# Memory attention plus a long convolution on one core: an evacuation engine chosen by the scheduler, masks as products in the last segment, and a tail without zero blocks

## The chip, the cores and the metric

The kernel runs on one core of one Trainium2 chip. The metric is the device time of one execution in microseconds (us). Three runs of the kernel before took 506.79, 511.01 and 514.14 us; the median is 511.01 us. The engines that matter are TensorE (PE, with its weight loads shown as PEld), VectorE (DVE), ScalarE (ACT) and SyncE (SP), which issues every DMA. GpSimd (POOL) does a few memsets.

## The reference

The input x has 2048 tokens of 512 numbers. Two branches are computed from x and mixed by a gate per token. All weights are bfloat16.

```python
g = sigmoid((x * gate_w).sum(-1, keepdims=True))
# A: 32 heads of 16, N = 4 segments of L = 512 tokens
logits = einsum('bhqd,bhkd->bhqk', qs, ks) * scale + mask      # per segment, causal
a_dot = einsum('bhqk,bhkd->bhqd', softmax(logits), vs)
a_mem = (phi(qs) @ M) / (phi(qs) @ z + 1e-6)                   # phi(t) = t+1 if t>0 else exp(t)
o = gh * a_mem + (1 - gh) * a_dot                              # gh = sigmoid(beta), per head
M, z = M + phi(ks)^T vs, z + sum(phi(ks))                      # carried to the next segment
a = o @ wo
# B: a state-space convolution; K from 128 complex states per channel
P = exp(dt * (A_re + 1j*A_im) * l)                             # l = 0..2047
K = einsum('dn,dnl,dn->dl', Cc, P, dB).real
b = irfft(rfft(pad(x)) * rfft(pad(K)))[:2048] + x * Dskip
out = g * a + (1 - g) * b
```

## The kernel before

Every engine instruction and DMA is an `Op` with a key (its due time), an engine, a cost and the tiles that it reads, writes and needs. `Sched.schedule` (L252) places all of them before the launch: it repeatedly takes, for each engine, the ready op with the lowest key that could start soon, and appends it to that engine's program. The result is one fixed order per engine. On the chip each engine runs its list in order and waits for semaphores; an instruction that waits holds up everything behind it on its engine. All DMAs are in one such list, on SP, issued at L249. All matmuls but the transposes are recorded at L720.

The keys come from `KEYS = (12, 6, 50, 70)` (L17): attention groups are due 12 apart from 6 on, the tables of the convolution start at 50 and are 70 apart, and the tail is due after the fourth table.

The pieces, with the lines that the text speaks of:

- **Powers** (`ssm_prep`, `ssm_powers`, L773 to L833): ACT and DVE square a complex number ten times, one step after the other, and store each power in the pool `pw`.
- **Attention** (L923 to L1117). Per segment of 512 tokens: V is projected and copied out of PSUM (L936); q and k are projected per group of 8 heads (`project`; q copied at L984, k twice with a head mask at L987 and L988). A `group` (L999) is 4 heads. It has 5 slots: 2 or 4 score products with 32 rows each; then 2 products of the identity with a block `negm` that adds -30000 above the diagonal (L1026); one exp on ACT over 128x1024 (L1032); and the products with V (17 columns) that add into `PV`, which is copied to `raw` (L1046). There are 32 groups, so 160 exps. `ophase` (L1051) transposes, normalises on DVE, adds the memory part and copies `oT` (L1099). `oproj` (L1102) multiplies by wo, scales by the gate (L1115) and writes `scr_abuf` to DRAM.
- **Gates** (`gate_tokens`, L897): after segment 3 the gate column goes to DRAM (`scr_gbuf`) and comes back in another layout; DVE reads it at L916.
- **Tables** (`tables(c)`, four times): 15 complex multiplies of three DVE instructions each (L1148, L1150, L1153) fill F and G with powers; 256 small products on PE (32 rows by 49 columns) make K samples, copied by ACT (L1195), written to `scr_K` in four DMAs and read back as one (L1199); DVE shuffles them (L1200, L1203), PE transposes them into `KTT`, ACT copies (L1213).
- **First Fourier step of x** (`x_level1`): products copied by ACT (L879) and DVE (L881) and written to `scr_Z`.
- **Tail** (`tail`, L1216). The constants `c_M2` and `c_N1` (2 MB each) and `scr_Z` are loaded (32 DMAs). Then 16 steps t: load a slice `c_D`; 10 products make K's spectrum (L1246), ACT copies (L1250); 16 products of 64 rows by 64 columns over 256 (L1261) make x's spectrum, ACT copies (L1267); DVE multiplies (L1271, L1273, L1275); 4 products with N1 (L1282) transform back; DVE or ACT in turn copy V (L1286, L1288) and it goes to `scr_V`. After every fourth t, `scr_V` is read back transposed into V2 by four DMAs (L1294).
- **End** (`fin`, L1298): four times: load x and `scr_abuf` pieces, u = x*Dskip on DVE (L1310), per quarter an identity product of u and two products with G2 and V2 (L1318 to L1320), one DVE instruction that mixes (L1324), four DMAs out.

Buffers that share memory belong to phases: Zx, M2, N1 and the rest of the tail's pools lie over F, G, t2 and `pw` (L686 to L695), and a pool can be used only when all pools under it are finished.

## Time and profile before

| | |
|---|---|
| runs | 506.79, 511.01, 514.14 us (median 511.01) |
| the profiled execution's own time | 510.9 us |
| its span | 509.1 us |
| mean granted clock of TensorE | 0.837 |
| PE busy | 376.7 us (74%), 3801 matmuls |
| DVE busy | 341.1 us (67%), 586 instructions |
| ACT busy | 310.8 us (61%), 397 instructions |
| DMA | 46.02 MB in 64489 packets |
| chain that ended last, by engine | PE 31%, DVE 28%, DMA 17%, ACT 12%, SP's queue 6%, issue 4% |

Read the shares of busy time as averages over stages with different limits: none of the engines is busy all the time, and each stage has its own one that ends last. [...] In a row of the timeline the brackets give how long the engine had been idle before and what released it.

### The profile page before, as it was taken

Reading aid. Unit: us, or ns where it says so; the run is one execution under the profiler, and the core shown is the slowest. Engines: PE = TensorE matmul, PEld = TensorE weight load, DVE = VectorE, ACT = ScalarE, POOL = GpSimd, SP = SyncE. Lnnn points to the kernel's source line nnn. Section 1 sums busy time; section 2 is a strip of 40 time slices with the busy share of each in tenths; the row PEclk is TensorE's granted clock in tenths of the full one; section 3 lists DMA queues with packets and bytes.
Section 4 is the critical chain, followed back from the end, with each engine's and each line's share of the span. In section 5 each row is a group of like instructions: output and inputs, shape, how many; then the busy total and the mean of one; then the engine's idle time right before and its main releaser. Section 6 shows DMA issues by size and latency. Waiting matters only on the chain.

```text
span 509.1 us, 9111 instructions
## 1 busy us (share of the span) xinstructions
PE 376.7 (74%) x3801; PEld 165.1 (32%) x3837; DVE 341.1 (67%) x586; ACT 310.8 (61%) x397; POOL 4.5 (1%) x17
## 2 busy tenths in 40 slices
PE   4873499999667976889877789647991898985370
PEld 3330133334333425334333233223341344432010
DVE  3777586999576897899965999432120878664074
ACT  4899986978556883586884639624581266554000
POOL 1000000000000000000000000000000000000000
PEclk9995555999895996999995989966587799999586
DMA  8600003222491101200015000059999757654546
GB/s 234 159 1 2 0 0 128 80 84 88 133 52 44 42 0 18 49 1 33 12 16 42 10 3 1 1 154 190 214 152 181 165 169 215 194 179 146 154 111 160
DMA packets 64489, 46.02 MB, mean 90 GB/s; under 512 B 28353, under 2 KB 59585, under 8 KB 64193
## 3 DMA queue, kind: packets, MB, share of 16 engines
q1 hardware_dynamic: 64448, 45.44, 40.2%
q8 instruction: 30, 0.49, 0.5%
q14 instruction: 11, 0.08, 0.1%
HBM read 31.23 MB, written 14.20 MB: 89 GB/s over the span
## 4 chain that ended last, share of the span: by engine, by line
PE 31%; DVE 28%; DMA 17%; ACT 12%; SPq 6%; issue 4%; DVEq 0%; ACTq 0%
PE psum L720 29%; SPq L249 6%; DVE sb L1153 5%; DVE sb L1150 5%; DVE sb L1148 4%; ACT sb L1032 3%; DMA scr_K<-sb 3%; DMA sb<-in_A_x_dram 2%; DMA scr_gbuf<-sb 2%; DMA scr_abuf<-sb 2%; DMA sb<-c_D 2%; ACT sb L819 2%; DMA sb<-scr_V 2%; DMA sb<-scr_K 1%; DVE sb L881 1%
## 5 line engine op out<-in xcount | busy, mean ns | idle before, releaser
L720 PE MATMUL psum<-sb 128*32 128x49 bf16 (+15 forms) x3565 | 357.1, 292 | 92.1 <-ACT sb L1032 17.1
L720 PEld LDWEIGHTS psum<-sb 128*128 128x128 bf16 (+5 forms) x3601 | 146.1, 101 | 298.3 <-issue 125.5
L1032 ACT ACTIVATE sb<-psum 128x1024 bf16<-128x1024 f32 x160 | 158.0, 1028 | 40.0 <-PE psum L720 38.5
L1153 DVE TENSOR_TENSOR sb<-sb 128x2048 bf16<-128x2048 bf16 (+3 forms) x60 | 51.8, 864 | 1.8
L1148 DVE TENSOR_TENSOR sb<-sb 128x2048 bf16<-128x2048 bf16 (+3 forms) x60 | 51.2, 857 | 0.1
L1150 DVE TENSOR_TENSOR sb<-sb 128x2048 bf16<-128x2048 bf16 (+3 forms) x60 | 51.3, 855 | 0.0
L1250 ACT ACTIVATE sb<-psum 128x1024 bf16<-128x1024 f32 x16 | 16.4, 1023 | 24.2 <-PE psum L720 24.2
L1115 ACT ACTIVATE sb<-psum,sb 128x512 bf16<-128x512 f32 x16 | 11.0, 687 | 24.5 <-PE psum L720 17.4
L1310 DVE TENSOR_TENSOR sb<-sb 128x2048 bf16<-128x2048 bf16 x4 | 9.1, 2289 | 19.4 <-PE psum L720 18.8
L1046 ACT ACTIVATE sb<-psum 128x512 bf16<-128x512 f32 x32 | 19.1, 597 | 2.8 <-PE psum L720 2.8
L1267 ACT ACTIVATE sb<-psum 128x1024 bf16<-128x1024 f32 x16 | 16.2, 1021 | 4.6 <-PE psum L720 4.6
L1064 DVE RECIPROCAL sb<-psum 128x32 f32<-128x32 bf16 x16 | 5.6, 352 | 19.4 <-PE psum L1059 19.4
L1059 PE MATMUL psum<-sb 128*128 128x128 bf16 x128 | 12.9, 260 | 7.2 <-ACT sb L1115 6.0
L1286 DVE CAST sb<-psum 128x1024 bf16<-128x1024 f32 x8 | 9.8, 1224 | 11.9 <-PE psum L720 11.9
L988 DVE TENSOR_SCALAR sb<-psum,sb 128x512 bf16<-128x512 f32 x16 | 11.9, 745 | 6.5 <-ACT sb L987 6.5
L1099 DVE CAST sb<-psum 128x512 bf16<-128x512 f32 x16 | 11.0, 687 | 7.4 <-PE psum L720 7.4
L1195 ACT ACTIVATE sb<-psum 128x392 bf16<-128x392 f32 x16 | 7.4, 501 | 13.5 <-PE psum L720 11.1
L881 DVE CAST sb<-psum 128x1024 bf16<-128x1024 f32 x8 | 9.8, 1223 | 7.0 <-PE psum L720 6.8
L1324 DVE SCALAR_TENSOR_TENSOR sb<-psum,sb 128x512 bf16<-128x512 f32 x16 | 10.8, 742 | 4.6 <-DMA out_dram<-sb 4.6
L1083 DVE TENSOR_SCALAR sb<-psum 128x32 f32<-128x32 f32 x12 | 2.2, 186 | 17.3 <-PE psum L720 17.3
L1059 PEld LDWEIGHTS psum<-sb 128*128 128x128 bf16 x128 | 10.5, 120 | 9.5 <-ACT sb L1115 6.2
L987 ACT ACTIVATE sb<-psum,sb 128x512 bf16<-128x512 f32 x16 | 11.0, 689 | 4.2 <-PE psum L720 4.1
(83 smaller groups left out, 257.4 us busy)
## 6 DMA issues: line engine op xcount, KB each, us to landing
sb<-c_D SPq DMA_DIRECT2D x16, 320.0 KB, 4.6
sb<-in_A_x_dram SPq DMA_DIRECT2D x32, 128.0 KB, 4.5
scr_Z<-sb SPq DMA_DIRECT2D x16, 256.0 KB, 2.1
sb<-scr_Z SPq DMA_DIRECT2D x32, 128.0 KB, 8.8
scr_V<-sb SPq DMA_DIRECT2D x16, 256.0 KB, 3.6
sb<-scr_V SPq DMA_DIRECT2D x16, 256.0 KB
sb<-in_A_x_dram SPq DMA_DIRECT2D x4, 512.0 KB, 4.3
scr_abuf<-sb SPq DMA_DIRECT2D x16, 128.0 KB, 2.6
```

The source lines that it names most:

```text
L249: return self.op("SP", 0.06, lambda e: e.dma_start(out(), in_(), **kw), r=r, w=w, pw=pw, key=key, lat=lat)
L720: mm = lambda e, o_, l, r_, st, sp, **kw: e.matmul(o_, lhsT=l, rhs=r_, start=st, stop=sp, skip_group_check=True, **kw)
L881: op("DVE", c_dps(1024), lambda e, P=P, zs=zs: e.tensor_copy(ap(zs, n=1024), ap(P, n=1024)), r=[P], w=[zs])
L988: op("DVE", c_dps(512), lambda e, P=P: e.tensor_scalar(ap(ko, n=512), ap(P, n=512), ap(mkT, 1, n=1), None, ALU.mult), r=[P, mkT], w=[ko])
L1032: op("ACT", c_act(1024), lambda e, P=P, pT=pT: e.activation(ap(pT, n=1024), ap(P, n=1024), ACT.Exp, scale=0.25), r=[P], w=[pT])
L1046: op("ACT", c_act(512), lambda e: e.activation(ap(raw, n=512), ap(PV, n=512), ACT.Copy), r=[PV], w=[raw])
L1059: i = e.transpose(ap(P, tb * 256 + gi * 128, n=128), ap(ra[gi], tb * 128, n=128), ap(ident, n=128))
L1148: op("DVE", c_tt(256 * n), lambda e: e.tensor_tensor(run(tile, ne, dst, 1), run(tile, ne, src, sstep), pwv(0), ALU.mult), r=rd + [pw], w=w ...
L1150: op("DVE", c_tt(256 * n), lambda e: e.tensor_tensor(run(t2, n, 0, 1), run(tile, ne, src, sstep), pwv(1), ALU.mult), r=rd + [pw], w=[t2])
L1153: op("DVE", c_tt(256 * n), lambda e: e.tensor_tensor(D_(), D_(), ap(t2, n * 128, [[-n * 128, 2], [2 * n, 64], [1, 2 * n]]), ALU.add), r=[t ...
L1250: op("ACT", c_act(1024), lambda e, PK=PK, K3=K3: e.activation(ap(K3, dims=[[1024, 2], [1, 512]]), ap(PK, dims=[[512, 2], [1, 512]]), ACT.C ...
L1267: op("ACT", c_act(1024), lambda e, PX=PX, Xs=Xs: e.activation(ap(Xs, dims=[[256, 2], [512, 2], [1, 256]]), ap(PX, dims=[[512, 2], [256, 2] ...
```

## The change

1. Copies out of PSUM that had a fixed engine (xT, parameters, V, q, both k, zs, `PV`, `oT`, the `oproj` result, kex, KTT, and in the tail K3, Xs, V) become ops with two alternatives (`evac`): the scheduler puts each on ACT or DVE while it builds the order. DVE's alternative carries a key 20 higher (`PEN`).
2. In the last segment (all 8 groups, `MASKD = 24`) the identity products that add `negm` are gone. After the exp a DVE multiply by a 0/1 block zeroes the masked parts of `pT` in place (40 multiplies).
3. The tail's data are laid out anew. M2 and N1 lose their zero blocks (1 MB each). `scr_Z` is loaded so that one product over 128 rows replaces two over 64: 4 products of 64 output columns over 512 in place of 16 over 256. The back transform becomes 8 products of 64x64 over 512, in pairs on the two diagonal quadrants, in place of 4 full ones. V goes to `scr_V` by two DMAs of 64 partitions per t, in runs of 1 KB, and comes back by two DMAs of 16 partitions per four t, in place of four of 8.
4. M2, N1 and the small tail buffers move over `pw`; the `c_D` slices move over G. There are 4 `c_D` slots (3 before), 3 Xs, 3 Y and 5 V.
5. `KEYS` are (11, 6, 60, 65). Some costs given to the scheduler change, and PE ops now acquire the destination tile of the copy that follows.

```diff
-KEYS = (12, 6, 50, 70)
+KEYS = (11, 6, 60, 65)
+    def evac(self, dst, src, n, r, w=(), pw=(), key=None, scale=None, psum16=False):
+        if scale is None:
+            fa = lambda e: e.activation(dst(), src(), ACT.Copy)
+            fd = lambda e: e.tensor_copy(dst(), src())
...
+        return self.op("ANY", 0.0, None, r=r, w=w, pw=pw, key=key,
+                       alts={"ACT": (0.17 + 0.000833 * n + ex, fa), "DVE": (0.15 + (0.00052 if psum16 else 0.00104) * n + ex / 2, fd)})
...
+        def push(o):
+            if o.alts:
+                for e_ in o.alts:
+                    ready[e_].append((o.key + (PEN if e_ == "DVE" else 0.0), o.seq, o))
...
         ZxP = mkpool("Zx", 32768, 1, 2)
-        M2P = mkpool("M2", 16384, 1, 2)
-        N1P = mkpool("N1", 16384, 1, 2)
-        DP = mkpool("Dst", 2560, 3, 2)
+        DP = mkpool("Dst", 2560, 4, 2)
+        a = T1
+        M2P = mkpool("M2", 8192, 1, 2)
+        N1P = mkpool("N1", 8192, 1, 2)
...
+            md = 8 * s + 2 * hg + gi >= MASKD
...
-                    for bk in range(2):
+                    for bk in (() if md else range(2)):
...
+                if md:
...
+                    op("DVE", c_tt(128 * len(offs)), lambda e, pT=pT, dims=dims: e.tensor_tensor(
+                        ap(pT, dims=dims + [[1, 128]]), ap(pT, dims=dims + [[1, 128]]),
+                        ap(mask01, dims=[[0, k_[1]] for k_ in dims] + [[1, 128]]), ALU.mult), r=[mask01], w=[pT])
...
-                for h in range(2):
-                    for i in range(4):
-                        S.dma(lambda h=h, i=i, zq=zq: ap(Zx, zq * 4096, [[256, 16], [1, 256]], p0=64 * h + 16 * i, np_=16),
-                              lambda h=h, i=i, zq=zq: bass.AP(Zd, zq * 16 * 2048 + i * 512 + h * 256, [[256 * 512, 16], [2048, 16], [1, 256]]),
+                for i in range(4):
+                    for c in range(2):
+                        S.dma(lambda c=c, i=i, zq=zq: sbp(Zx, 64 * c + i, 4, 16, [[512, 8], [1, 512]], zq * 4096),
+                              lambda c=c, i=i, zq=zq: bass.AP(Zd, zq * 8 * 4096 + c * 2048 + i * 512, [[256 * 512, 16], [4096, 8], [1, 512]]),
...
-                        for ci in range(2):
-                            for pi in range(2):
-                                for h in range(2):
-                                    p = 2 * t + pi
-                                    i = mm(e, ap(PX, h * 512 + co * 256, n=256, p0=64 * pi, np_=64),
...
+                        for pi in range(2):
+                            p = 2 * t + pi
+                            i = mm(e, ap(PX, co * 512, n=512, p0=64 * pi, np_=64), ap(M2, p * 128 + co * 64, n=64),
+                                   ap(Zx, p * 512, n=512), True, True, tile_position=(0, 64 * pi))
...
-                            i = mm(e, ap(PI, co * 512, n=512), ap(N1, ((t * 2 + ci) * 2 + co) * 128, n=128), ap(Y, ci * 512, n=512), ci == 0, ci == 1)
+                            for pi in range(2):
+                                cx = co if pi == 0 else 1 - co
+                                i = mm(e, ap(PI, cx * 512, n=512, p0=64 * pi, np_=64), ap(N1, ((t * 2 + ci) * 2 + cx) * 64, n=64, p0=64 * pi, np_=64),
+                                       ap(Y, ci * 512, n=512, p0=64 * pi, np_=64), ci == 0, ci == 1, tile_position=(64 * pi, 64 * pi))
...
+                for pi in range(2):
+                    S.dma(lambda t=t, pi=pi: bass.AP(Vd, (2 * t + pi) * 65536, [[512, 64], [32768, 2], [1, 512]]),
+                          lambda V=V, pi=pi: ap(V, dims=[[512, 2], [1, 512]], p0=64 * pi, np_=64), 131072, r=[V], pw=[dV[t // 4]])
...
-                        for c in range(2):
-                            S.dma(lambda bl=bl, c=c, k=k: sbp(V2, 64 * bl + 32 * c + k, 4, 8, [[512, 32], [1, 512]]),
-                                  lambda bl=bl, c=c, k=k: bass.AP(Vd, k * 4 * 131072 + bl * 1024 + c * 512, [[65536, 8], [2048, 32], [1, 512]]),
-                                  262144, r=[dV[k]], pw=[V2])
+                        S.dma(lambda bl=bl, k=k: sbp(V2, 64 * bl + k, 4, 16, [[512, 32], [1, 512]]),
+                              lambda bl=bl, k=k: bass.AP(Vd, k * 8 * 65536 + bl * 512, [[32768, 16], [1024, 32], [1, 512]]),
+                              524288, r=[dV[k]], pw=[V2])
```

What the scheduler makes of it is seen in the engines' lists. The first place is SP's list from the copies of the last `oproj` of segment 2 to the read of the fourth table's K samples (`sb<-scr_K`); before the change it is

```order
L249 DMA sb<-c_D 128x1280 x3
L249 DMA sb<-c_N1 128x8192
L249 DMA scr_abuf<-sb 128x512
L249 DMA scr_K<-sb 128x8x49 x3
L249 DMA sb<-c_M2 128x8192
L249 DMA sb<-scr_Z 16x16x256 x8
L249 DMA scr_K<-sb 128x8x49
L249 DMA sb<-scr_Z 16x16x256 x15
L249 DMA scr_abuf<-sb 128x512
L249 DMA sb<-scr_Z 16x16x256 x9
L249 DMA sb<-scr_K 128x1568
```

and with the change, in the same place,

```order
L252 DMA sb<-c_M2 128x4096
L252 DMA sb<-c_N1 128x4096
L252 DMA scr_K<-sb 128x8x49 x3
L252 DMA sb<-c_D 128x1280 x2
L252 DMA sb<-scr_Z 16x8x512 x7
L252 DMA scr_K<-sb 128x8x49
L252 DMA sb<-scr_Z 16x8x512 x25
L252 DMA sb<-c_D 128x1280 x2
L252 DMA sb<-scr_K 128x1568
```

All 32 loads of `scr_Z` still stand ahead of the read of `scr_K`, each with 128 runs of 1 KB in place of 256 of 512 B; the two constants, half as long, come before the K samples are written.

The second place is SP's list at the end, from the last V writes to the first results; before:

```order
L249 DMA scr_V<-sb 128x1024 x4
L249 DMA scr_abuf<-sb 128x512 x2
L249 DMA sb<-scr_V 8x32x512 x4
L249 DMA scr_abuf<-sb 128x512 x2
L249 DMA sb<-scr_abuf 32x4x512 x12
L249 DMA out_0_dram<-sb 32x4x512 x4
```

and with the change:

```order
L252 DMA scr_V<-sb 64x2x512 x2
L252 DMA scr_abuf<-sb 128x512 x2
L252 DMA scr_V<-sb 64x2x512 x2
L252 DMA sb<-scr_abuf 32x4x512 x8
L252 DMA scr_V<-sb 64x2x512 x4
L252 DMA sb<-scr_V 16x32x512 x2
L252 DMA sb<-scr_abuf 32x4x512 x4
L252 DMA out_0_dram<-sb 32x4x512 x4
```

Eight of the sixteen `scr_abuf` loads now stand ahead of the last V writes; before, all stood behind the last V read.

The third place is DVE's list around the gate column of segment 3 (L910, L911 and L916 before; L929, L930 and L935 now). Before:

```order
L910 TENSOR_SCALAR sb<-sb 128x4
L911 RECIPROCAL sb<-sb 128x4
L1153 TENSOR_TENSOR sb<-sb 128x128x16
L1099 CAST sb<-psum 128x512
L1148 TENSOR_TENSOR sb<-sb 128x128x16
L1150 TENSOR_TENSOR sb<-sb 128x2048
L1153 TENSOR_TENSOR sb<-sb 128x128x16
L916 TENSOR_SCALAR sb<-sb 128x16
```

and with the change:

```order
L1060 TENSOR_TENSOR sb<-sb 128x2x128
L1060 TENSOR_TENSOR sb<-sb 128x2x2x128
L1060 TENSOR_TENSOR sb<-sb 128x2x128
L1060 TENSOR_TENSOR sb<-sb 128x2x2x128
L1060 TENSOR_TENSOR sb<-sb 128x4x128
L1177 TENSOR_TENSOR sb<-sb 128x128x8
L1179 TENSOR_TENSOR sb<-sb 128x1024
L1182 TENSOR_TENSOR sb<-sb 128x128x8
L1012 TENSOR_SCALAR sb<-sb 128x512
L1013 TENSOR_SCALAR sb<-sb 128x512
L1177 TENSOR_TENSOR sb<-sb 128x128x8
L935 TENSOR_SCALAR sb<-sb 128x16
```

L929 and L930 stand directly ahead of these rows. The five masks of a group (L1060) stand in DVE's list one behind the other, and the reader of the gate column still stands a few instructions behind its producer.

## Rows read from the trace of the kernel before

**Rows 1.** Stretches: busy us (count) of PE, PEld, DVE, ACT, POOL; clock; DMA share; GB/s

```profile
0.00:63.50 63.50, 36.31 (x257) 16.84 (x263) 39.59 (x80) 54.78 (x82) 2.15 (x9) 0.81 0.32 79
63.50:337.00 273.50, 221.68 (x2470) 98.15 (x2492) 221.95 (x373) 185.83 (x237) 2.37 (x8) 0.86 0.21 40
...
344.50:385.60 41.10, 36.78 (x297) 14.93 (x296) 9.15 (x25) 25.55 (x30) 0.00 (x0) 0.68 1.17 180
385.60:397.60 12.00, 0.73 (x6) 0.59 (x7) 2.27 (x9) 0.70 (x1) 0.00 (x0) 0.58 1.08 177
397.60:466.50 68.90, 60.30 (x454) 27.11 (x461) 50.67 (x79) 37.53 (x39) 0.00 (x0) 0.97 0.61 181
466.50:478.90 12.40, 2.34 (x11) 0.88 (x9) 0.00 (x0) 2.59 (x4) 0.00 (x0) 0.76 0.45 148
478.90:509.10 30.20, 13.25 (x47) 3.47 (x48) 15.30 (x18) 0.00 (x0) 0.00 (x0) 0.73 0.55 139
```

**Rows 2.** Groups by form: a table multiply of 512 elements, and the exp

```profile
L1150 DVE TENSOR_TENSOR sb<-sb 128x512 bf16<-128x512 bf16 x8 | 3.4, 422 | 0.0
...
L1032 ACT ACTIVATE sb<-psum 128x1024 bf16<-128x1024 f32 x160 | 158.0, 1028 | 40.0 <-PE psum L720 38.5
```

**Rows 3.** Timeline of DVE: start, us, instruction, [idle before and its releaser]

```profile
335.04 0.18 DVE L916 TENSOR_SCALAR sb<-sb 128x16 f32<-128x16 f32 x1 [11.01 <-DMA sb<-scr_gbuf]
```

**Rows 4.** Timeline of SP's queue, from the fourth table's K writes to their read

```profile
341.51 7.41 SPq L249 DMA_DIRECT2D scr_K<-sb  x3
...
349.57 11.81 SPq L249 DMA_DIRECT2D sb<-scr_Z  x8
...
363.82 12.60 SPq L249 DMA_DIRECT2D sb<-scr_Z  x15
...
385.03 1.18 SPq L249 DMA_DIRECT2D sb<-scr_K  x1
```

**Rows 5.** Timeline of DVE: the first reader of those K samples

```profile
394.87 0.16 DVE L1200 COPY sb<-sb 128x1 bf16<-128x1 bf16 x1 [9.11 <-DMA sb<-scr_K]
```

**Rows 6.** DMA issues on SP: ns least/median/most, first and last start

```profile
L249 SPq DMA_DIRECT2D sb<-scr_Z x32: 440/680/6124, 349.6 to 383.9; - x32
L249 SPq DMA_DIRECT2D sb<-in_A_x_dram x10: 312/432/433, 386.2 to 399.5; - x10
...
L249 SPq DMA_DIRECT2D sb<-scr_V x16: 639/652/762, 420.1 to 470.8; - x16
```

**Rows 7.** Timeline of weight loads in a group of segment 3: mask, then V product

```profile
357.45 0.13 PEld L720 LDWEIGHTS psum<-sb 128*128 128x128 bf16 x2 [0.41 <-issue]
...
357.98 0.09 PEld L720 LDWEIGHTS psum<-sb 128*17 128x17 bf16 x2 [0.41 <-issue]
```

**Rows 8.** Timeline of PE and its weight loads in the tail's 16 steps

```profile
412.24 0.36 PEld L720 LDWEIGHTS psum<-sb 64*64 64x64 bf16 x16 [0.42 <-issue]
...
412.80 1.84 PEld L720 LDWEIGHTS psum<-sb 128*128 128x128 bf16 x10 [0.20 <-issue]
...
416.12 7.22 PE L720 MATMUL psum<-sb 128*128 128x512 bf16 x59 [0.42 <-DVE sb L1275]
...
449.96 6.57 PE L720 MATMUL psum<-sb 128*128 128x512 bf16 x56 [1.41 <-DMA sb<-c_D]
```

**Rows 9.** Timeline of the end: V's last read, weight loads, the mixing

```profile
468.71 2.75 SPq L249 DMA_DIRECT2D sb<-scr_V  x4
...
478.91 2.28 PE L720 MATMUL psum<-sb 128*128 128x512 bf16 x6 [10.07 <-DMA sb<-scr_V]
...
483.89 0.10 PEld L720 LDWEIGHTS psum<-sb 128*128 128x128 bf16 x1 [0.23 <-issue]
484.21 0.11 PEld L720 LDWEIGHTS psum<-sb 128*64 128x64 bf16 x2 [0.23 <-issue]
...
488.19 5.35 DVE L1324 SCALAR_TENSOR_TENSOR sb<-psum,sb 128x512 bf16<-128x512 f32 x8
...
500.83 2.73 DVE L1324 SCALAR_TENSOR_TENSOR sb<-psum,sb 128x512 bf16<-128x512 f32 x4 [1.38 <-DMA out_dram<-sb]
```

More of the change, by code (lines that the diff above doesn't have):

```diff
@@ L128 @@
     __slots__ = ("eng", "cost", "fn", "deps", "key", "tiles", "wt", "nd", "succ", "start", "fin", "idx", "inc",
-                 "val", "sem", "know", "waits", "seq", "lat", "alld", "tag")
+                 "val", "sem", "know", "waits", "seq", "lat", "alld", "tag", "alts")
 class Sched:
@@ L335, in schedule @@
             o = choice[e][3]
-            ready[e].remove((o.key, o.seq, o))
+            if o.alts:
+                for e_ in o.alts:
+                    ready[e_] = [r_ for r_ in ready[e_] if r_[2] is not o]
+                o.eng = e
+                o.cost, o.fn = o.alts[e]
+            else:
+                ready[e].remove((o.key, o.seq, o))
             for T in o.tiles:
@@ L491, in fft_consts @@
     cs, sn = np.cos(th), np.sin(th)
-    rows = np.array([4 * b4 + i for i in range(4) for b4 in range(16)])
     m2 = np.zeros((64, 32, 2, 2, 64))
@@ L497, in fft_consts @@
     m2[:, :, 1, 1, :] = cs.transpose(1, 0, 2)
-    m2 = m2[rows]
-    M2 = np.concatenate([m2, m2], 0)
-    N1 = np.zeros((128, 16, 2, 2, 128))
+    M2 = m2.transpose(2, 0, 1, 3, 4).reshape(128, 32, 2, 64)
+    N1 = np.zeros((128, 16, 2, 2, 64))
     for t in range(16):
@@ L960, in f @@
                         return i
-                    op("PE", c_mm(136, 8), f, r=[vpad[s]] + [t for tb in range(4) for t in ekr[(s, tb)]], pw=[P])
+                    op("PE", c_mm(136, 8), f, r=[vpad[s]] + [t for tb in range(4) for t in ekr[(s, tb)]], pw=[P], acq=[Mx[s + 1]])
                 acc = lambda hp=hp: ap(accT, hp * 272, n=272)
@@ L1028, in f @@
                     return i
-                cost = 0.30 + 0.06 * len(ent)
                 pT = Tile(pTP, BF16)
-                op("PE", cost, f, r=[qT, ke, ko, ident, negm], w=[P], acq=[pT])
+                op("PE", 0.33 if md else 0.63, f, r=[qT, ke, ko, ident, negm], w=[P], acq=[pT])
                 op("ACT", c_act(1024), lambda e, P=P, pT=pT: e.activation(ap(pT, n=1024), ap(P, n=1024), ACT.Exp, scale=0.25), r=[P], w=[pT])
+                if md:
+                    offs = [bk * 512 + off for (_, _, bk, off) in ent]
+                    if len(offs) == 2:
+                        dims = [[512, 2]]
+                    elif 384 in offs:
+                        dims = [[512, 2], [384, 2]]
+                    else:
+                        dims = [[512, 2], [256, 2]]
+                    op("DVE", c_tt(128 * len(offs)), lambda e, pT=pT, dims=dims: e.tensor_tensor(
+                        ap(pT, dims=dims + [[1, 128]]), ap(pT, dims=dims + [[1, 128]]),
+                        ap(mask01, dims=[[0, k_[1]] for k_ in dims] + [[1, 128]]), ALU.mult), r=[mask01], w=[pT])
                 def g(e, pT=pT, ent=ent, seen0=dict(seen)):
@@ L1098, in ophase @@
             op("PE", c_mm(128, 4 * len(srcs)), f3, r=srcs + [ident], w=[P3], acq=[oT])
-            op("DVE", c_dps(512), lambda e: e.tensor_copy(ap(oT, n=512), ap(P3, n=512)), r=[P3], w=[oT])
+            S.evac(lambda: ap(oT, n=512), lambda: ap(P3, n=512), 512, r=[P3], w=[oT])
             oTs[(s, hg)] = oT
@@ L1329, in tail, with sbp @@
                           lambda ou=ou, i=i: ap(ou, p0=32 * i, np_=32, dims=[[512, 4], [1, 512]]), 131072, r=[ou])
-        def sbp(T, p0, pstep, np_, dims):
+        def sbp(T, p0, pstep, np_, dims, off=0):
             v = S.sb16[:]
@@ L1334, in sbp @@
             base = (T.pool.addr + T.slot * T.pool.size) // 2
-            return bass.AP(v.tensor, v.offset + p0 * st + base, [[pstep * st, np_]] + [list(d) for d in dims])
+            return bass.AP(v.tensor, v.offset + p0 * st + base + off, [[pstep * st, np_]] + [list(d) for d in dims])
         S.key = 0.0
```

113 lines of the change are left out of this document (53 added, 60 removed).

## Prediction

> **What bounds the kernel now.** I read the busy time by stretches first [rows 1], then, inside each stretch, the timeline of the engine that ends it. All times are of the profiled execution: 509.1 us of span, 510.9 us with what lies around it, against a median of 511.01 us, so the sum can be made against 510.9. Five stretches matter.
>
> (a) 0 to 63.5 us: ACT is busy 54.78 of 63.5 us with the powers, one after the other; DVE has 24 us free. (b) 63.5 to 337 us, the four tables with most of the attention under them: DVE is busiest in sum (221.95 of 273.5 us), PE equals it (221.68), ACT has 88 us free. The largest single gap is DVE's 11.01 us at L916, which waits for the gate column to come back from DRAM with everything on DVE behind it [rows 3]. (c) 341.5 to 397.6 us: the fourth table's K samples are written from 341.51 us on and are read by DVE only at 394.87 us [rows 4, 5], because their read stands in SP's queue behind 32 loads of `scr_Z`. PE works off the rest of the attention until 385.6 us at a granted clock of 0.68, and then is busy 0.73 of 12 us [rows 1]. (d) 397.6 to 466.5 us, 16 tail steps: PE is busy 60.30 of 68.9 us at a clock of 0.97; two steps take 7.22 + 0.42 = 7.64 us [rows 8], so PE is the bound. (e) 466.5 us to the end: PE waits 10.07 us for the last V read; the products start at 478.91 us, but the mixing instruction L1324 starts only at 488.19 us [rows 9], since the `scr_abuf` loads stand behind that read in SP's queue.
>
> **The change, part by part**
>
> *Copies on either engine, new keys, and the masks on DVE* (stretches a and b). By the order, DVE has between the first table's first copy and the last table multiply 27 copies out of PSUM where it had 55, and 25 of the 40 mask multiplies, which are new. At the stretch's mean of 221.95/373 = 0.60 us, 28 fewer copies are 17 us; most are larger than the mean, say 20 us. A mask has 256 or 512 elements; 25 at up to 0.42 us [rows 2] are 10 us. A few more normalisations bring 2 us. DVE's work falls by 8 us. Fifteen copies more come before the tables, into DVE's 24 free us of stretch a. ACT takes over about 28 copies and, by the order, 10 exps more before the table products end (150 against 140): some 17 + 10 us against 88 us free. PE gets 10 slots more and 25 mask steps less. So stretch b ends 8 us earlier if DVE bounds it. The unknown is how a new order of 9,000 instructions fits: DVE's free time in b is 51.5 us, 11 of it the wait for the gate column, which stays (the new order has 12 instructions between producer and reader). If half of the other 40 us went, the gain would be 8 + 20 = 28; if DVE fitted half as badly again, the loss would be 12. I take -8, ends -20 and +12.
>
> *scr_Z in longer runs* (stretch c). SP needs 0.68 us for one `scr_Z` load of 256 runs and 0.652 for one `scr_V` read of 256 runs, but 0.432 for an x load of 128 [rows 6]. The new loads have 128 runs. From the first K write to the reader, now 394.87 - 341.51 = 53.4 us. Then: three K writes 7.4 [rows 4], the fourth 2.5, 32 Z loads at 0.43 = 13.8, four `c_D` at no more than 0.43 = 1.7, the read's issue 1.2; 26.6 us of issue. The landing took 394.87 - 386.2 = 8.7 us behind a full queue; with 2 MB less of constants ahead of it I take 4. Sum 31, that is -22. If a Z load goes on costing 0.68, it is 34.6 + 8.7 = 43, -10. The cover is PE's attention: it was busy 36.78 us here. 3 of 5 groups of V products are left, 10 of 20 score slots, no masks; a step takes 0.53 us at half clock [rows 7], so 25 steps in place of 65, about 13 us, with two output phases, half an `oproj` and three of x's spectra (some 8 us) about 21: less than 31, so the chain of K remains the bound. I take -21, ends -10 and -24.
>
> *Tail products* (stretch d). x's spectrum: 16 products took 0.56 us, from the first weight load to the next form's [rows 8]. A full product of 512 columns takes 0.21 us (ten weight loads in a row span 1.84 + 0.20 us [rows 8]), so 16 x 256 columns one after the other would be 1.7 us: they run three at a time. Four products of 512 columns in pairs are 2 x 0.21 = 0.42 us plus a change of form. The two G2 products at the end, the same form, take with the step before them 0.32 us from weight load to weight load [rows 9], 0.11 over one pass: that is the price of a change of form. The back transform has 8 products in place of 4; in pairs they are 4 passes as before. One change of form more per step: 16 x 0.11 = +1.8. No copy is the bound: DVE has 50.67 of 68.9 us. Four `c_D` slots should take away the wait of 1.41 us [rows 8], perhaps a shorter one too. Half of the last `oproj` and the last output transpose leave the tail: 8 products of 0.2 us, 1.6. Sum -2; ends -5 and, if the diagonal pairs do not run together, 16 x 4 x 0.21 = +13.4.
>
> *V back and the end* (stretch e). The last read takes from 468.71 to 478.91, 10.2 us [rows 9], and the DMA share stands at 0.45 [rows 1], while the 16-partition loads of `scr_Z` had 1.17: half of the engines idle. With 16 partitions per read I take -4, +0.5 for the second V write; ends -6 and 0. [...] The mixing then starts after the first products, not 9.3 us after them; the two L1310 that hid in this gap come out at 2 x 2.3 us. -9.3 + 4.6 = -4.7, and a little of L1310 still lies beside PE: -6; ends -8 and -2.
>
> Sum: -8 - 21 - 2 - 3.5 - 6 = -40.5, 510.9 - 40.5 = **470 us**.
>
> **Rivals**
>
> 1. *DVE's queue waits for exps.* A group's five masks stand one behind the other on DVE, and an exp takes 1.03 us [rows 2] against 0.42 for a mask: up to 5 x 0.6 = 3 us lost per group, 8 groups, 24 us, with table multiplies behind them. For: DVE is the bound of b. Against: the order puts other work between groups, and seven `pT` buffers let exps run ahead. 470 + 24 = 494 us. Chance 0.12.
>
> 2. *The diagonal pairs do not run together.* 470 + 13.4 + 2 = 485 us. Against: the old 64x64 form did [rows 8], though on all four quadrants. Chance 0.10.
>
> 3. *The change doesn't do what it says for `scr_Z`.* The 16 DMA engines were full (share 1.17 [rows 1]) while Z was loaded; if the bytes and not the runs fill them, the 4 MB land no sooner, the chain of K gains 6 and not 21 us (2 MB of constants at 180 GB/s are 11 us, half of them ahead), and an order as good as the old one, not better, gives nothing in b: 510.9 - 6 - 2 - 3.5 - 6 = 493 us. Chance 0.11. [...]
>
> 4. *Slower: the tail runs at half clock.* The stretch where PE was busy 36.78 of 41.1 us had a clock of 0.68 [rows 1], so a busy PE is not always granted 1.0; there it had products of 32 rows and of 17 columns. The back transform now fills two quadrants instead of all. If the clock fell to 0.5 throughout the 16 steps, each would take 3.6 us more (PE's 7.22 us per two steps [rows 8]): +58, 528 us. It decides from about three quarters of the steps on. Against: 10 of the 16 passes of a step are the unchanged 128-row products, and the tail had 0.97. Chance 0.04.
>
> **The numbers.** My forecast, 470, has a chance of 0.60; the four rivals 0.37; 0.03 is for an order that loses all elsewhere and ends within 2%. The range takes the ends of the first two terms together on the good side (470 - 12 - 3, and 5 for the rest: 450) and reaches over rivals 1 to 3 on the other: 450 to 497. Left out are rival 4, part of rival 1 with a bad fit in b, and a little below, under 0.2. Runs of this kernel differ by 1.4%, so 2% is what can be told from none: faster means below 500.8, slower above 521. Faster: 0.60 + 0.10 + 0.10 + 0.07 = 0.87; same 0.08; slower 0.05.
>
> **What would show it.** The reader of K's samples (L1229 now) within 31 us of the first K write, not 53; the last table multiply near 329 us; `scr_Z` issues of 0.43 us; a tail step of 3.8 us at a clock of 0.95 or more; the mixing within 2 us of the first end products; the wait at L935 still near 11 us. Wrong would be: waits of DVE for exps at L1060 of over 10 us in sum, `scr_Z` issues of 0.68, or PE waits in the back transform.

## The result and the profile after

The changed kernel takes 489.8 us (median of four runs, 486.03 to 490.55) against 508.97 us (506.79 to 514.14) for the kernel before in the same comparison: a ratio of 0.9595, 95% interval 0.950 to 0.969. It is faster, by about half of what was forecast. Runs of one kernel differ by some per cent, and one that is over 1.5% above the fastest of its kernel is left out of a ratio but not of a median or a range. The profiled execution has a span of 488.0 us, 21.1 less than the one before.

The stretches of the kernel after, in the columns of [rows 1], cut at the same events: powers; tables up to the first write of the fourth table's K; from there to the reader of K; the tail up to the last step's multiplies; the last V bounce; the end.

```profile
0.00:63.50 63.50, 44.97 (x293) 20.44 (x299) 49.02 (x96) 54.05 (x80) 2.15 (x9) 0.92 0.42 113
63.50:338.90 275.40, 228.77 (x2705) 98.06 (x2726) 216.44 (x387) 209.01 (x274) 2.37 (x8) 0.81 0.21 36
338.90:377.90 39.00, 22.01 (x214) 10.36 (x205) 11.26 (x30) 16.83 (x22) 0.00 (x0) 0.62 0.94 208
377.90:443.50 65.60, 61.88 (x333) 23.06 (x341) 51.83 (x80) 34.42 (x35) 0.00 (x0) 0.95 0.79 198
443.50:459.00 15.50, 1.96 (x17) 0.59 (x13) 1.99 (x3) 2.05 (x2) 0.00 (x0) 0.72 0.75 169
459.00:488.00 29.00, 13.87 (x47) 3.49 (x48) 15.49 (x18) 0.00 (x0) 0.00 (x0) 0.68 0.41 109
```

The same events before and after, in us, before and after from one profile each; the differences add up to the 21.1:

| stretch | before | after | difference | forecast |
|---|---|---|---|---|
| start to first K write | 341.5 | 338.9 | -2.6 | -8 |
| first K write to reader | 53.4 | 39.0 | -14.4 | -21 |
| reader to the last step's first multiply | 67.4 | 65.6 | -1.8 | -2 |
| from there to the first end product | 16.6 | 15.5 | -1.1 | -3.5 |
| first end product to first mixing | 9.3 | 1.2 | -8.1 | -9.3 |
| first mixing to the end | 20.9 | 27.8 | +6.9 | +3.3 |

The first row is the least certain: three later profiles with the same order up to there have the first K write at 331.88 (e3), 336.08 (e11) and 338.45 us (e8), so it could as well read -9.6.

Most of the gain is in the chain of K. Its SP queue after, which answers to [rows 4], and the reader, which answers to [rows 5]:

```profile
338.91 4.98 SPq L252 DMA_DIRECT2D scr_K<-sb  x3
344.31 1.34 SPq L252 DMA_DIRECT2D sb<-c_D  x2
345.69 6.25 SPq L252 DMA_DIRECT2D sb<-scr_Z  x7
351.99 0.59 SPq L252 DMA_DIRECT2D scr_K<-sb  x1
352.62 18.02 SPq L252 DMA_DIRECT2D sb<-scr_Z  x25
370.69 1.06 SPq L252 DMA_DIRECT2D sb<-c_D  x2
371.91 0.32 SPq L252 DMA_DIRECT2D sb<-scr_K  x1
...
377.91 0.16 DVE L1229 COPY sb<-sb 128x1 bf16<-128x1 bf16 x1 [7.58 <-DMA sb<-scr_K]
```

The 32 `scr_Z` loads hold SP for 6.25 + 18.02 = 24.27 us, 0.76 each; before it was 11.81 + 12.60 [rows 4] and 7.68 for the last nine, 32.09 us:

```profile
377.19 7.68 SPq L249 DMA_DIRECT2D sb<-scr_Z  x9
```

The read lands 6.0 us after its issue.

On DVE the wait for the gate column is still there, 25 us earlier than in [rows 3], and masks stand between the table multiplies behind it (timeline of DVE; the last row is the last table multiply):

```profile
309.97 0.17 DVE L935 TENSOR_SCALAR sb<-sb 128x16 f32<-128x16 f32 x1 [11.67 <-DMA sb<-scr_gbuf]
...
326.19 0.42 DVE L1060 TENSOR_TENSOR sb<-sb 128x512 bf16<-128x512 bf16 x1 [1.55 <-ACT sb L1051]
...
335.35 0.39 DVE L1182 TENSOR_TENSOR sb<-sb 128x256 bf16<-128x256 bf16 x1
```

The end, which answers to [rows 9] (timelines of SP, PE and DVE):

```profile
443.31 3.65 SPq L252 DMA_DIRECT2D sb<-scr_abuf  x8
447.00 2.53 SPq L252 DMA_DIRECT2D scr_V<-sb  x4
451.38 1.21 SPq L252 DMA_DIRECT2D sb<-scr_V  x2
...
459.00 7.40 PE L745 MATMUL psum<-sb 128*128 128x512 bf16 x24 [12.34 <-DMA sb<-scr_V]
...
460.22 0.75 DVE L1349 SCALAR_TENSOR_TENSOR sb<-psum,sb 128x512 bf16<-128x512 f32 x1 [14.67 <-PE psum L745]
461.33 0.75 DVE L1349 SCALAR_TENSOR_TENSOR sb<-psum,sb 128x512 bf16<-128x512 f32 x1 [0.36 <-PE psum L745]
463.54 2.29 DVE L1335 TENSOR_TENSOR sb<-sb 128x2048 bf16<-128x2048 bf16 x1 [1.46 <-PE psum L745]
466.44 2.29 DVE L1335 TENSOR_TENSOR sb<-sb 128x2048 bf16<-128x2048 bf16 x1 [0.61 <-PE psum L745]
468.65 4.04 DVE L1349 SCALAR_TENSOR_TENSOR sb<-psum,sb 128x512 bf16<-128x512 f32 x6
475.72 2.72 DVE L1349 SCALAR_TENSOR_TENSOR sb<-psum,sb 128x512 bf16<-128x512 f32 x4 [3.04 <-DMA out_dram<-sb]
```

The mixing starts 1.2 us after the first end product, but after two of a group's four mixings DVE takes the two late L1335, u for the third and fourth groups. The first group's output leaves only at 471.86 us, and the third group waits for its buffer.

### The profile page after: what moved, and what is told of

It is laid out like the page before. It is cut to its first block, busy times and chain, and to the rows that moved or that the text cites. A ratio compares the mean times of both kernels' runs of the same rounds, so it can differ in the third digit from the quotient of the medians.

```text
span 488.0 us, 8740 instructions
## 1 busy us (share of the span) xinstructions
PE 373.5 (77%) x3593; PEld 156.0 (32%) x3629; DVE 346.0 (71%) x612; ACT 316.4 (65%) x411; POOL 4.5 (1%) x17
## 4 chain that ended last, share of the span: by engine, by line
PE 34%; DVE 24%; DMA 14%; ACT 13%; SPq 8%; issue 4%; DVEq 0%
PE psum L745 33%; SPq L252 8%; DVE sb L1182 6%; DVE sb L1179 6%; ACT sb L1051 5%; DVE sb L1177 5%; DMA scr_K<-sb 4%; ACT sb L256 3%; DMA sb<-scr_K 2%; DMA scr_gbuf<-sb 2%; DMA sb<-scr_V 1%; ACT sb L841 1%; DMA scr_abuf<-sb 1%; DMA sb<-in_A_wq_dram 1%; DVE sb L1097 1%
## 5 line engine op out<-in xcount | busy, mean ns | idle before, releaser
L745 PE MATMUL psum<-sb 128*32 128x49 bf16 (+13 forms) x3357 | 355.0, 302 | 84.0 <-issue 14.9
L745 PEld LDWEIGHTS psum<-sb 128*128 128x128 bf16 (+4 forms) x3393 | 138.6, 101 | 296.0 <-issue 123.7
L1051 ACT ACTIVATE sb<-psum 128x1024 bf16<-128x1024 f32 x160 | 157.4, 1029 | 21.2 <-PE psum L745 20.7
L256 ACT ACTIVATE sb<-psum 128x512 bf16<-128x512 f32 (+4 forms) x137 | 98.7, 741 | 92.3 <-PE psum L745 81.9
L257 DVE CAST sb<-psum 128x1024 bf16<-128x1024 f32 (+1 forms) x34 | 34.1, 1003 | 25.9 <-PE psum L745 25.8
L259 ACT ACTIVATE sb<-psum,sb 128x512 bf16<-128x512 f32 x35 | 23.9, 687 | 11.1 <-PE psum L745 9.5
L1060 DVE TENSOR_TENSOR sb<-sb 128x512 bf16<-128x512 bf16 (+1 forms) x40 | 13.2, 367 | 7.8 <-ACT sb L1051 7.7
L841 ACT ACTIVATE sb<-sb 128x1024 bf16<-128x1024 f32 x11 | 11.7, 1064 | 0.0
L1335 DVE TENSOR_TENSOR sb<-sb 128x2048 bf16<-128x2048 bf16 x4 | 9.1, 2292 | 3.6 <-PE psum L745 2.1
L1295 DVE TENSOR_TENSOR sb<-sb 128x1024 bf16<-128x1024 bf16 x16 | 11.1, 693 | 0.6
L1299 DVE TENSOR_TENSOR sb<-sb 128x1024 bf16<-128x1024 bf16 x16 | 11.1, 692 | 0.6
L1097 DVE TENSOR_TENSOR sb<-psum,sb 128x512 bf16<-128x512 bf16 x16 | 11.1, 691 | 0.5
L1297 DVE TENSOR_TENSOR sb<-sb 128x1024 bf16<-128x1024 bf16 x16 | 11.0, 685 | 0.0
```

The lines of the kernel that those rows point to most:

```text
L256: fa = lambda e: e.activation(dst(), src(), ACT.Copy)
L257: fd = lambda e: e.tensor_copy(dst(), src())
L259: fa = lambda e: e.activation(dst(), src(), ACT.Copy, scale=scale())
L745: mm = lambda e, o_, l, r_, st, sp, **kw: e.matmul(o_, lhsT=l, rhs=r_, start=st, stop=sp, skip_group_check=True, **kw)
L841: op("ACT", c_act(1024), lambda e, pw=pw, zr=zr: e.activation(ap(pw, 0, [[512, 4], [128, 2], [1, 128]]), ap(zr, 0, [[128, 4], [0, 2], [1, ...
L1051: op("ACT", c_act(1024), lambda e, P=P, pT=pT: e.activation(ap(pT, n=1024), ap(P, n=1024), ACT.Exp, scale=0.25), r=[P], w=[pT])
```

## The experiments

Each was compared with the kernel before, whose median lay between 507.27 and 509.26 us in these comparisons; a difference to the changed kernel's 489.8 us is one between two comparisons, and no finer than these 2 us. All edits are to the changed kernel unless the text says otherwise.

**e1, the tail alone, by way of the changed kernel.** Old engines, keys and masks.

```diff
-MASKD = 24
-KEYS = (11, 6, 60, 65)
+MASKD = 32
+KEYS = (12, 6, 50, 70)
-        return self.op("ANY", 0.0, None, ..., alts={...})
+        cost, fn = {"ACT": (...), "DVE": (...)}[eng]     # eng as before the change
+        return self.op(eng, cost, fn, ...)
```

> The changed kernel with the old engine for each PSUM copy, the old keys and all masks on TensorE; tail products, scr_Z loads, V bounce and the loads of the end stay new. Theory A (the re-laid tail carries the gain: 14 of the 21 us between the first K write and the reader of K, 2 at the end): about 17 us below the kernel before, 490 to 496 us, K write to reader about 39 us. Rival B (the placement and the masks carry it, because attention is over earlier): 3 to 6 us below the kernel before, 503 to 508 us, K write to reader 48 us or more.

521.31 us, ratio 1.032 (1.023 to 1.041): both theories missed. First K write to reader is 39.6 us (359.63 to 399.2), as A said, but the first K write comes 18 us later than before. With the old engines and keys the order of the table stretch is still not the old one (products also claim the buffer of their copy when they are placed, `acq`), but a third. That the order alone costs the 18 us is likely, not shown. The layout alone had to be tried in the old order, which is e5.

**e5, the tail alone, in the kernel before.**

```diff
 # kernel before
-        (constants, pools, tail() of the kernel before)
+        (constants, pools, tail() of the changed kernel; copies on ACT, V on DVE and ACT in turn)
```

> The kernel before with the new tail alone (x spectrum, back transform, scr_Z loads, V bounce, constants, four c_D slots); its order on DVE up to the end of the tables is the old one. Theory A (the re-laid tail carries most of the gain, e1 lost only through another order in the table stretch): first K write near 341 us, reader about 40 us behind it, 490 to 496 us. Rival B (the tail gives little without the new order around it): 503 to 509 us, reader 48 us or more behind the first K write.

498.71 us, ratio 0.982 (0.974 to 0.991): the layout alone is worth some 8.6 us, by the interval 5 to 13. The time lies between the two theories. First K write to reader is 39.5 us (336.93 to 376.4), 13.9 less than before, as A said; the profile is 18.5 us ahead at the reader and 11.7 at the end, so 6.8 are lost later. In the old order the last attention group ends inside the tail, and on DVE two u instructions (4.49 us) stand between the multiplies of the last step (timeline of DVE in e5, then of PE):

```profile
444.57 0.69 DVE L1271 TENSOR_TENSOR sb<-sb 128x1024 bf16<-128x1024 bf16 x1
445.18 4.49 DVE L1311 TENSOR_TENSOR sb<-sb 128x2048 bf16<-128x2048 bf16 x2
449.58 0.69 DVE L1273 TENSOR_TENSOR sb<-sb 128x1024 bf16<-128x1024 bf16 x1
...
451.05 1.91 PE L725 MATMUL psum<-sb 64*64 64x512 bf16 x8 [6.01 <-DVE sb L1275]
```

**e4, no masks on DVE.**

```diff
-MASKD = 24
+MASKD = 32
```

> The changed kernel with all masks as TensorE products with negm, none as a multiply on DVE. Theory A (in the table stretch DVE and PE both have slack or trade even): 487 to 492 us. Rival B (the masks taken from PE pay: 40 steps of 0.5 us at half clock): 495 us or more. Rival C (the multiplies cost DVE more than they save): 480 to 485 us.

477.81 us (475.84 to 479.31), ratio 0.942 (0.938 to 0.947): 12 us below the changed kernel, beyond C's range. The first K write comes 18.3 us earlier; from there to the reader it is 38.9 us as before the edit (timeline of SP in e4, then in e3, whose order there is the changed kernel's):

```profile
320.61 6.28 SPq L252 DMA_DIRECT2D scr_K<-sb  x3
```

```profile
331.88 4.97 SPq L253 DMA_DIRECT2D scr_K<-sb  x3
```

So the three parts of the change are worth, by medians and put in one after the other: layout -8.6 (e5), engines and keys with the rest of point 5 477.8 - 498.7 = -20.9, masks on DVE +12.0. Three edits then ask where the 12 come from.

**e6, both masks.** The multiplies stay; 72 mask products are back on TensorE, in the same order.

```diff
-            ... len(dg[bk]) == 0, md, tile_position=(32 * r, 0))
+            ... len(dg[bk]) == 0, False, tile_position=(32 * r, 0))
-                    for bk in (() if md else range(2)):
+                    for bk in range(2):
```

> The changed kernel, instruction for instruction, with the 24 mask steps on TensorE put back beside the multiplies on DVE (a masked entry is masked twice, the result is the same): 72 more products in the same order. Theory A (the late attention runs at half clock because TensorE has less to do; more products raise the granted clock): clock over 260 to 340 us up from 0.50 to 0.76 to 0.75 and more, first K write at most 334 us, 480 to 486 us. Rival B (the multiplies on DVE are what costs, TensorE's work only adds): clock the same, 24 steps of 0.25 to 0.53 us more, 491 to 500 us.

488.33 us, ratio 0.966 (0.960 to 0.972), as the changed kernel. The clock did go up, but no time came of it. The windows from 260 to 340 us, of the changed kernel and then of e6:

```profile
260.00:340.00 80.00, 55.06 (x578) 22.09 (x580) 56.13 (x115) 51.47 (x68) 0.00 (x0) 0.62 0.22 31
```

```profile
260.00:340.00 80.00, 61.77 (x581) 25.28 (x586) 56.51 (x117) 51.19 (x65) 0.00 (x0) 0.72 0.20 24
```

The mean granted clock is 0.72 for 0.62 (0.83 in the kernel before and 0.79 in e4, same window), and the first K write comes at 340.52 us instead of 338.91. So A is wrong as far as this rise goes, and B's 491 to 500 us are not seen either: within the runs' spread the mask products on TensorE cost nothing here, and taking them away saved nothing.

**e7, multiplies of 8 columns.**

```diff
-                        ap(pT, dims=dims + [[1, 128]]), ...
+                        ap(pT, dims=dims + [[1, 8]]), ...       # in and out, and mask01
```

The kernel leaves out most of each mask.

> The changed kernel, instruction for instruction, with the multiplies cut from 128 to 8 columns of each block (the mask is left unfinished): same order and waits, about 0.3 us less on DVE for each of 40 multiplies, 24 groups of columns or 10 us in sum. Theory A (DVE's time for the masks is what costs): first K write 6 to 10 us earlier, 479 to 484 us. Rival B (the clock costs, DVE's time does not): 486 to 490 us.

484.71 us (481.51 to 489.28), ratio 0.955 (0.949 to 0.961): between A's range and B's, 5 us below the changed kernel by medians, and the intervals of the two ratios overlap. The first K write, 335.04, is inside the spread of the unedited order (331.88 to 338.91). The multiplies now take 0.17 us, but DVE's waits for exps at L1060 grow from 7.7 to 11.1 us in sum. The multiply's own time is at most about half of the 12 us.

**e10, no multiplies, in the changed kernel's own order.** As e6, and the multiplies, placed as before, are not issued; who waited for one waits for its exp.

```diff
+                    mo.skip = True          # mo: the multiply, placed but not issued
+        self.prog = {e: [o for o in l if not o.skip] for e, l in self.prog.items()}
```

> The changed kernel in its own order with the masks as products on TensorE and the 40 multiplies taken out of DVE's queue (as e6 without the multiplies; as e4 in its work, not in its order). Theory A (the multiplies and DVE's waits for exps that come with them cost the 12 us that e4 gained): first K write 321 to 327 us, 475 to 480 us. Rival B (the order of e4 brings most of it): first K write 332 to 338 us, 483 to 488 us.

484.2 us, ratio 0.942 (0.934 to 0.950). The five runs lie between 475.82 and 487.49 us, and the ratio rests on the two shortest, 475.82 and 479.13, which are A's times and those of e4. The other three, 484.2 to 487.49, are B's. The trace is of the longest, so it can't say what the shortest do. The two speak for A, that the multiplies and their waits cost the 12 us and not the order; how much the order of the products on PE adds stays open.

**e2, the read of K ahead of the loads of the tail.** `od` places an operation behind another without a wait.

```diff
-            S.dma(lambda: ap(M2, n=4096), ..., w=[M2])
+            S.dma(lambda: ap(M2, n=4096), ..., w=[M2], od=[kread[3]])     # and N1, scr_Z, c_D
```

> The changed kernel with the read of the fourth table's K samples ahead of all loads of the tail in SP's queue (M2, N1, scr_Z, c_D). Theory A (SP's queue holds the reader back): first K write to reader at most 20 us instead of 39.0, tail products about 10 us earlier, 475 to 482 us. Rival B (the transfers fill the DMA engines, and the first x spectra then wait for scr_Z and M2 as long as the K read waited): 486 to 492 us, PE waiting for scr_Z where it waited for K. Rival C (PE's attention is what ends last there): reader early, tail start within 3 us of the old one, 485 to 490 us.

484.79 us, ratio 0.955 (0.951 to 0.959): rival C, a little below its range. Timelines of SP, DVE and PE:

```profile
336.51 2.62 SPq L253 DMA_DIRECT2D scr_K<-sb  x4
348.00 0.33 SPq L253 DMA_DIRECT2D sb<-scr_K  x1
...
351.00 0.16 DVE L1232 COPY sb<-sb 128x1 bf16<-128x1 bf16 x1 [5.40 <-DMA sb<-scr_K]
...
378.71 21.48 PE L746 MATMUL psum<-sb 128*128 128x512 bf16 x103 [0.69 <-ACT sb L257]
```

The reader comes 14.5 us after the first K write, and still the unbroken row of products begins at 378.71 us, against 380.28 in the changed kernel. PE had attention steps, waits for `scr_Z` and for the constant N1 until then; some tail steps were done in between, and the last products end 8 us earlier. Counted from the first K write, the row begins no earlier than in the changed kernel (42.2 us against 41.4): with the reader early, PE's other work and its waits end last.

**e11, each scr_Z load split in two.**

```diff
-                        S.dma(... [[512, 8], [1, 512]] ..., 131072, ...)
+                        for h in range(2):
+                            S.dma(... [[512, 8], [1, 256]] ..., 65536, ...)
```

> The changed kernel with each scr_Z load split into two of half the columns: 64 loads of 128 runs of 512 B in place of 32 of 128 runs of 1 KB, the same bytes, twice the runs. Theory A (the bytes fill the DMA engines, and SP's queue only waits for them): 0.33 to 0.42 us of SP's queue for each load, 21 to 27 us in sum as before the split (24.3), reader 38 to 42 us behind the first K write, 487 to 492 us. Rival B (each run or each load has its price): 0.55 to 0.75 us each, 35 to 48 us in sum, reader 50 us or more behind, 498 to 510 us.

507.9 us, ratio 1.003 (0.999 to 1.007): B, and the whole gain is gone. The reader is at 394.06 us, 58.0 behind the first K write. Timeline of SP, and the window around its long row:

```profile
348.63 37.73 SPq L252 DMA_DIRECT2D sb<-scr_Z  x57
```

```profile
348.60:386.40 37.80, 14.09 (x98) 5.56 (x94) 7.61 (x19) 11.31 (x14) 0.00 (x0) 0.63 0.41 112
```

0.66 us a load, with the DMA engines at a share of 0.41: SP's queue is the bound, not the engines. Runs and loads were doubled together, so one more run parts them.

**e12, 16 scr_Z loads of twice the size.**

```diff
-            for zq in range(4):     # [[512, 8], [1, 512]], 131072 bytes
+            for zq in (0, 2):       # [[512, 16], [1, 512]], 262144 bytes
```

> The changed kernel with 16 scr_Z loads of 256 runs of 1 KB in place of 32 of 128: the same runs and bytes, half the loads (the split of e11 doubled runs and loads together). Theory A (each load has its price in SP's queue, 0.66 us with the DMA engines a third busy in e11): until the engines fill, 16 loads at 0.66 to 1.1 us, 11 to 17 us in sum instead of 24.3, reader 28 to 33 us behind the first K write instead of 39.0, 478 to 484 us. Rival B (the price goes by runs, 5.3 to 5.9 ns each): 1.35 to 1.5 us a load, 22 to 24 us in sum, reader 37 to 40 us behind, 486 to 492 us.

486.96 us, ratio 0.955 (0.946 to 0.965), in B's range; the profiled run is the longest of four, 489.59 us. The reader is 41.9 us behind the first K write (337.30 to 379.25). The sum of the loads is 5.00 + 10.10 = 15.1 us, as A said; the reader is not. The issues on SP, in the columns of [rows 6], of the changed kernel, e11 and e12:

```profile
L252 SPq DMA_DIRECT2D sb<-scr_Z x32: 571/600/2104, 345.7 to 370.0; - x32
```

```profile
L252 SPq DMA_DIRECT2D sb<-scr_Z x64: 597/600/1612, 342.5 to 385.8; - x64
```

```profile
L252 SPq DMA_DIRECT2D sb<-scr_Z x16: 571/610/3102, 345.7 to 361.1; - x16
```

And of e12 the end of SP's row, DVE at the reader, and a window of the last nine loads:

```profile
362.82 3.75 SPq L252 DMA_DIRECT2D sb<-in_A_x_dram  x8
366.73 0.34 SPq L252 DMA_DIRECT2D sb<-scr_K  x1
...
374.84 4.49 DVE L1335 TENSOR_TENSOR sb<-sb 128x2048 bf16<-128x2048 bf16 x2 [6.24 <-DMA sb<-in_A_x_dram]
379.25 0.15 DVE L1229 COPY sb<-sb 128x1 bf16<-128x1 bf16 x1
```

```profile
351.50:361.70 10.20, 4.53 (x42) 1.44 (x41) 2.95 (x7) 5.31 (x7) 0.00 (x0) 0.73 1.07 251
```

The median issue is 0.60 us for 128 runs of 1 KB, for 128 of 512 B, and 0.61 for 256 of 1 KB: a price of the load, not of its runs. With half the loads the engines fill (share 1.07), and the read of K, now also behind eight x loads, lands 10.9 us after its issue instead of 6.0. It lands at 377.7 us, and the reader then waits until 379.25 behind two u instructions, which stand ahead of it in this order and had waited for the x loads. So what SP gave up went to the engines and, 1.6 us, to DVE's order.

**e3, the scr_abuf loads behind the last scr_V writes.**

```diff
-                          131072, r=dA, pw=[aj], key=k0 + 50)
+                          131072, r=dA, pw=[aj], key=k0 + 50, od=[vlast])
```

> The changed kernel with the scr_abuf loads of the mixing behind the last scr_V writes in SP's queue. Theory A (SP's wait for the scr_abuf writes holds back the last four scr_V writes): these four issues start about 3.5 us earlier after the last product than 447.0 against 445.6, the last V read lands 3 to 5 us earlier, 484 to 487 us. Rival B (the end is paced by its two u, aj and ou buffers, whatever the V read does): 487 to 490 us.

486.67 us (484.80 to 489.57), ratio 0.960 (0.955 to 0.966), as the changed kernel. The time is A's, the mechanism B's: the eight loads (3.88 us) now stand between the last V writes and the V read, the read is issued 9.7 us after the last step's first multiply instead of 7.9, and 29.6 us pass from the first end product to the end, 29.0 in the changed kernel. Up to the last step the order is that of the changed kernel, yet this profile's first K write is at 331.88 us and not 338.91: so much two executions of one order differ in the table stretch.

**e8, more buffers at the end.**

```diff
-uP, ajP, ouP: 2, 2, 2 buffers
+uP, ajP, ouP: 4, 4, 3 buffers
-                          131072, r=dA, pw=[aj], key=k0 + 50)
+                          131072, r=dA, pw=[aj], key=k0 + 50, od=[last scr_V read])
```

> The changed kernel with four u, four aj and three ou buffers at the end in place of two each, and the scr_abuf loads behind the last scr_V read. Theory A (the end is paced by its buffers and by the two u instructions among the first mixings on DVE): from the first end product to the end 20 to 22 us instead of 29, 479 to 483 us. Rival B (TensorE at half clock, 16 steps of 0.9 us, or the output writes pace it): 27 to 29 us, 487 to 490 us.

477.58 us, ratio 0.945 (0.938 to 0.952): A, a little below its ranges, 12 us less than the changed kernel. From the first end product, 456.54 us, to the end, 476.0, it is 19.5 us. The buffers and the order of the loads were changed together; behind the V writes alone the loads brought nothing (e3). No u instruction stands in the mixing any more (timeline of DVE):

```profile
458.83 2.07 DVE L1350 SCALAR_TENSOR_TENSOR sb<-psum,sb 128x512 bf16<-128x512 f32 x3 [15.05 <-PE psum L746]
461.07 0.75 DVE L1350 SCALAR_TENSOR_TENSOR sb<-psum,sb 128x512 bf16<-128x512 f32 x1 [0.17 <-PE psum L746]
462.38 8.10 DVE L1350 SCALAR_TENSOR_TENSOR sb<-psum,sb 128x512 bf16<-128x512 f32 x12 [0.55 <-PE psum L746]
```

**e9, together.** The edits of e4, e2 and e8, and the instruction that waits for the gate column placed late:

```diff
-                op("DVE", ..., ap(omg4T, n=16), ..., w=[omg4T])
+                op("DVE", ..., ap(omg4T, n=16), ..., w=[omg4T], key=1000.0)
```

> The changed kernel with four edits: all masks on TensorE (e4), the K read ahead of the loads of the tail (e2), the buffers and the load order of the end (e8), and, new, the instruction at L935 that waits for the gate column put late in DVE's order. Theory A (the single gains of 12, 5 and 12 us add up, and DVE's wait of 11 us at L935 goes): 449 to 456 us. Rival B (they overlap, since with the K read early TensorE bounds the way into the tail, and DVE's wait was slack): 460 to 468 us.

454.9 us (450.5 to 457.24), ratio 0.897 (0.890 to 0.904): A's range, 35 us below the changed kernel. The gate's wait is gone, but the first K write, 320.35 us, is where e4 had it (320.61): that wait was slack in this stretch, as B said. The other three act in stretches that follow one another, and in the profiles their gains add up: the first K write is 18.6 us earlier than in the changed kernel, the first end product 22.9, the end 32.6. The row of tail products begins 41.7 us after the first K write, as in e2. The medians differ by 35 us, 6 more than the 12, 5 and 12 of the single edits; these 6 have no test. From the reader of K to the last step's multiplies, and from there to the end:

```profile
335.20:420.70 85.50, 79.55 (x505) 30.90 (x505) 59.85 (x98) 52.26 (x56) 0.00 (x0) 0.96 0.87 230
420.70:455.40 34.70, 13.85 (x56) 3.77 (x56) 12.14 (x19) 1.02 (x1) 0.00 (x0) 0.70 0.89 200
```

## Why the prediction was right in direction and half too large

**Tables, forecast -8, seen -2.6.** The failing step is "A mask has 256 or 512 elements; 25 at up to 0.42 us are 10 us", which counts the masks' own time and nothing with it. That time was right: 0.285 and 0.421 us each, 9.1 us for the 25 up to the last table multiply. The larger form in the changed kernel:

```profile
L1060 DVE TENSOR_TENSOR sb<-sb 128x512 bf16<-128x512 bf16 x24 | 9.9, 421 | 7.7 <-ACT sb L1051 7.7
```

But up to the first K write 30 masks take 11.0 us of DVE and bring waits for exps of 3.7 us, with table multiplies behind them; and from the first K write of the third table to that of the fourth it is 67.4 and 64.2 us without masks on DVE (e4, e9) and 78.6 to 81.8 in four profiles with them (the changed kernel, e3, e8, e11). So the masks cost 11 to 18 us there. That is rival 1's mechanism at a part of its price; its sign, waits at L1060 over 10 us, was not met (7.7), so the sign was set for the rival's full size. The other side of the term is near the 20 worked out: copies on either engine with the new keys bring 16 us in this stretch (336.93 in e5, 320.61 in e4, one profile each). And "PE gets ... 25 mask steps less" counted for nothing (e6). As executions of one order differ by 7 us here, the -8 may have been met; then a larger cost of the masks was made up by a gain that was not counted, such as the 4.6 us that the first K write is earlier with the layout alone (e5), and that would be luck. The medians of e4 and e5 carry the parts, not the two profiles.

**Chain of K, forecast -21, seen -14.4; e5 shows -13.9 for the layout alone.** The failing step is "The new loads have 128 runs", so 0.43 us. The x load's 0.43 [rows 6] does not carry over: in the new layout a `scr_Z` load holds SP 0.60 or 0.61 us by the median, whatever it carries (e11, e12), and 0.76 on the mean in the changed kernel. 32 of these are 24.3 us instead of 13.8, 10.5 more; shorter K writes (5.57 us for four against 9.9 assumed) give a part back. The step "so the chain of K remains the bound" holds only in part, too: with the reader 14.5 us after the first K write (e2), the row of tail products begins no earlier after that write, and the kernel gains 5 us. Of what before shows, the 0.68 was close to this price, and its mean of 1.00 held the engines' share: full, as rival 3 said. So rival 3 was right in what bounds the kernel before, and wrong in what follows: with the new loads the engines are no longer the only bound. Windows of the last row of loads, in the kernel before and after:

```profile
363.80:385.00 21.20, 19.39 (x179) 7.44 (x180) 3.41 (x9) 16.01 (x18) 0.00 (x0) 0.76 1.23 158
```

```profile
352.60:370.70 18.10, 9.87 (x78) 4.36 (x77) 6.54 (x15) 8.23 (x10) 0.00 (x0) 0.56 0.85 218
```

The share is 1.23 before and 0.85 after. Full engines moved 158 GB/s with runs of 512 B (before) and 251 with 1 KB (e12, share 1.07), other transfers included, 1.6 times as much. That the length of the runs does this is not shown. The loads before also write 16 adjacent partitions each and the new ones every fourth partition, and in e11 runs of 512 B in the new places moved 112 GB/s at a share of 0.41, an estimated 270 at a share of 1 (112/0.41) against some 130 before (158/1.23).

**Tail steps, forecast -2, seen -1.8.** Right, with a step of 3.82 us (16 first multiplies, 386.2 to 443.5 us) at a granted clock of 1.00; over the whole stretch from 377.9 us its mean was 0.95. The diagonal pairs do run together: 120 products in the form 64x64 took 15.8 us, 0.13 each, where one alone would take 0.21 (2.04 us for ten [rows 8]). Rival 2 is out, and so is rival 4.

```profile
L745 PE MATMUL psum<-sb 64*64 64x512 bf16 x120 | 15.8, 382 | 1.3 <-DVE sb L1299 1.3
```

**V read and end, forecast -9.5, seen -2.3.** The read takes 7.6 us instead of 10.2, -2.6 of the -4. That reads of 8 partitions leave half of the DMA engines idle, on which the -4 rests, no run shows; from the read's issue to the first end product the DMA share was 0.43 before (468.71 to 478.91 us) and 0.69 after (451.38 to 459.00 us), at 141 and 138 GB/s, other transfers included. The writes ahead of the read gave 1.5 back, for which the `scr_abuf` loads ahead of them account at most in half (without them, in e8, 14.8 us instead of 15.5). The mixing did start at once (1.2 us). The failing step is "the two L1310 that hid in this gap come out at 2 x 2.3 us": their time was right, their place was not. They cut the first group's mixing in two, so that its output, and with two buffers each all later groups, went 7 us later. e8, which takes this away, gains 12 us, some 10 of them between the first end product and the end (19.5 us against 29.0).

**Signs.** Reader within 31 us: no, 39.0. Last table multiply near 329: no, 335.4. Issues of 0.43: no, and near the 0.68 that was to show it wrong. Step, clock, mixing within 2 us, L935 near 11 us: yes. PE's waits in the back transform, which were to show it wrong, were 2.5 us, all in the last two steps. ("12 instructions between producer and reader" are 11 by the list; nothing hangs on it.)
